# Weights' factor inside the split, four small operations off VectorE, wide filler products

## The chip, the cores and the metric

The kernel runs on one core of a Trainium2 chip. Its engines each work through a queue of their own, in order: TensorE (PE; its weight loads are listed as PEld), VectorE (DVE), ScalarE (ACT), GpSimd (POOL), and SyncE (SP), which only issues transfers here. The metric is the device time of one launch in microseconds (us); lower is better.

## What is computed

Three stages follow each other. The first is attention over chunks of 32 queries (4 batches, 8 heads, 768 positions, 64 columns a head), each chunk seeing 8 memory keys and 56 neighbours. Its result, 3072 tokens of 512 columns, goes through a layer with SoLU (h times softmax of h), a layer norm with a factor `g_ln` for each of 1024 inner columns, and then through a second layer with 2048 inner columns.

```python
a = np.exp(scores - np.max(scores, axis=-1, keepdims=True))
a = a / (np.sum(a, axis=-1, keepdims=True) + 1e-09)
...
h = x @ w_in
e = np.exp(h - h_max)
solu = h * (e / (np.sum(e, axis=-1, keepdims=True) + 1e-09))
ln = (solu - mu) / np.sqrt(var + 1e-06) * g_ln
x = ln @ w_out
...
h = x @ w2_in
out = (h * np.clip(h + 3.0, 0.0, 6.0) / 6.0) @ w2_out
```

The weights arrive as 64-bit numbers; the kernel makes 32-bit ones of them with bit operations.

## The kernel before

The tokens are cut into 24 tiles of 128. Each big product is made of three fp32r products: an operand is split into a high part (`hi`, the value rounded to fp32r) and a low part (`lo`, the rest), and hi times hi, hi times lo and lo times hi are summed.

The work of the first stages is written out by hand as lists of steps. `FIRST` holds everything up to the point where the pipeline is full (tiles 0 to 6 through SoLU, up to tile 8 through attention, and the conversion of the first layer's weights, `w1_*`, and of the SoLU layer's second weights, `wo_*`). `BODY` is one period of the loop over tiles 7 to 23, `LAST` and `CHANGE` lead into the last layer. An entry `name:args` calls a function that issues instructions; every engine takes its instructions in the order of the list, so an instruction waits for all those that stand ahead of it on its engine.

The steps that matter here, for a tile i:

- `k_p:i,half` transposes the keys of a tile on TensorE, two pairs of heads in a call; each pair takes a transpose of 128 rows (`kn`) and one of 24 rows (`km`). `k_e` (mostly ScalarE) copies the result to `kT`, a single buffer until tile 9, so it waits for the scores of the tile before. `q_p`, `q_e` do the same for the queries (`qb`).
- `s_p` makes the scores (PSUM tile `sc`), `s_max`, `s_sub`, `s_exp`, `s_sum` the softmax up to 1/(sum + 1e-9), `s_norm` multiplies by it (`pn`), `p_p` transposes that, `p_e` copies it to `pb`, `v_p` multiplies by the values, `x_h` and `x_l` split the result, `m1` makes h.
- `ln_max`, `ln_exp`, `ln_den`, `ln_solu`, `ln_mean`, `ln_sq`, `ln_var`, `ln_pow`, `ln_norm` are SoLU and the layer norm; `ln_p` transposes, `ln_h` and `ln_l` split, `m2` multiplies by the second weights.
- `wo_abs`, `wo_hold`, `wo_bits` convert a block of the second weights, `wo_g` multiplies it by `g_ln`, `wo_hi` and `wo_lo` split it.
- `warm:n` puts n products on TensorE whose result nobody reads; they fill waits.

Transposes and their evictions share three PSUM buffers (`tp`), the scores have one (`sc`).

Of the kernel before, what the change touches and what calls it, by code (L numbers as in the profile page):

```python
# [8 lines left out]
F32 = mybir.dt.float32  # L9
F32R = mybir.dt.float32r  # L10
# [25 lines left out]
    s_norm:1,P spread_mem_v:0,0,A q_p:3 load_q:4 k_e:3,1,A warm:2 v_p:0 w1_lo:7,D k_e:3,0,A q_e:3,1,A s_max:2 k_p:4,1
    q_e:3,0,D w1_bits:5,2 w1_hi:6,A w1_lo:6,P w1_hi:5,A w1_lo:5,P s_sub:2 x_h:0,0 x_l:0,0 load_w1:3 s_exp:2 p_p:1
    p_e:1,0,A w1_abs:1,A p_e:1,1,A s_p:3 k_p:4,0 k_e:4,0,A k_e:4,1,A m1:0,1,0 s_sum:2 s_norm:2,D q_p:4 p_p:2 load_v:1
    w1_hold:1,P load_w1:2 s_max:3 s_sub:3 q_e:4,1,A m1:0,1,1 w1_bits:1,0 w1_abs:3,D w1_bits:1,1 w1_bits:1,2 w1_hi:1,D
    load_k:5 w1_lo:1,D q_e:4,0,A spread_mem_v:1,0,A s_p:4 spread_mem_v:1,64,A v_p:1 x_h:1,0 load_q:5 w1_hold:3,P  # L40
    w1_bits:3,0 p_e:2,0,A w1_bits:3,1 consts w1_abs:2,A x_l:1,0 w1_bits:3,2 w1_hold:2,D load_v:2 load_wo:7 p_e:2,1,A
    m1:0,0,0 w1_bits:2,0 w1_bits:2,1 early_open m1:1,0,0 w1_bits:2,2 w1_hi:3,A w1_hi:2,A w1_lo:2,P load_k:6 s_exp:3
    w1_lo:3,D k_p:5,1 k_e:5,1,D q_p:5 q_e:5,0,A k_p:5,0 k_e:5,0,A q_e:5,1,A s_max:4 load_g s_sum:3 s_norm:3,D m1:1,1,0
    s_sub:4 s_exp:4 m1:0,0,1 load_wo:4 ln_max:0 ln_exp:0 s_sum:4 ln_den:0 ln_solu:0 v_p:2 s_p:5 wo_abs:7,A s_edge:5
    wo_abs:4,A wo_hold:7,D x_h:2,0 k_p:6,1 m1:1,0,1 x_l:2,0 k_e:6,1,D load_q:6 load_wo:5 wo_hold:4,D ln_mean:0 p_p:3
# [1334 lines left out]
```

## Time and profile before

| | |
|---|---|
| median of 3 runs | 867.32 us (866.62 to 868.14) |
| the profiled execution, its own time | 867.68 us |
| its span, first to last instruction | 865.9 us |
| TensorE busy | 858.0 us (99%) |
| VectorE busy | 747.1 us (86%) |
| ScalarE busy | 469.7 us (54%) |
| GpSimd busy | 259.3 us (30%) |
| mean granted TensorE clock | 0.996 of 2.4 GHz |

The busy time of TensorE is made of modelled ends of pipelined matmuls, so that 99% says only that it has hardly a gap; how fast it goes through its work is read from the distance of the starts. Times in the timeline are counted from the first instruction.

### The profile page before, as it was taken

The page shows a single profiled execution, that of the slowest core. Times are in us where ns is not written, and L with a number is a line of the kernel's source. Part 1 is how long each engine was busy: PE and PEld are TensorE (multiplying, and loading weights), DVE is VectorE, ACT ScalarE, POOL GpSimd, SP SyncE. Part 2 cuts the span into 40 slices and gives each one's busy share as a digit, 9 for nine tenths or more (in the row PEclk, how much of TensorE's full clock was granted, in tenths as well). Part 3 has the DMA queues.
Part 4 walks back from the last instruction along what each step waited for, and adds up shares of the span by engine and source line. Part 5 has one row for each costly group of instructions (what it writes and reads, how often), then busy time and mean ns, then how long its engine had stood idle before and what let it go on. Part 6 is the DMA issues. An engine that isn't in the chain of part 4 may idle for free.

```text
span 865.9 us, 20130 instructions
## 1 busy us (share of the span) xinstructions
PE 858.0 (99%) x7513; PEld 811.9 (94%) x7513; DVE 747.1 (86%) x1599; ACT 469.7 (54%) x865; POOL 259.3 (30%) x228
## 2 busy tenths in 40 slices
...
GB/s 239 188 219 160 72 144 225 236 230 302 240 275 224 268 274 231 145 163 228 251 191 148 225 136 207 178 173 226 240 262 255 166 135 142 158 141 135 140 141 62
DMA packets 184014, 168.27 MB, mean 194 GB/s; under 512 B 107116, under 2 KB 154220, under 8 KB 183916
## 3 DMA queue, kind: packets, MB, share of 16 engines
...
q10 hardware_dynamic: 288, 0.26, 0.1%
...
## 4 chain that ended last, share of the span: by engine, by line
PE 88%; DVE 6%; ACT 2%; DMA 2%; issue 1%; SPq 0%; DVEq 0%; ACTq 0%
PE acc L903 25%; PE acc L990 24%; PE m L694 15%; PE h L609 12%; PE tp L666 3%; PE sc L522 3%; PE tp L578 2%; PE tp L560 1%; PE tp L509 1%; PE tp L494 1%; DMA w1raw<-in_moe_w_in_dram 1%; DMA b_ll<-b_d 1%; PE tp L480 1%; DMA f_z<-g 1%; ACT e L644 0%
## 5 line engine op out<-in xcount | busy, mean ns | idle before, releaser
L694 PE MATMUL m<-lnh,wo 128*128 128x384 f32 x512 | 138.5, 344 | 0.0
L938 ACT ACTIVATE f_s<-f_e,constants 128x512 f32<-128x512 f32 x96 | 68.0, 720 | 74.2 <-DVE f_e L931 60.4
L609 PE MATMUL h<-w,xh 128*128 128x512 f32 x336 | 106.4, 398 | 0.0
L694 PEld LDWEIGHTS m<-lnh,wo 128*128 128x128 f32 x512 | 91.7, 188 | 0.2
L694 PE MATMUL m<-lnl,wo 128*128 128x384 f32 x256 | 88.0, 344 | 0.0
L311 POOL TENSOR_SCALAR w2t<-w2t 128x512 f32<-128x512 f32 x30 | 58.8, 1961 | 53.6 <-ACT w2t L304 53.6
L609 PEld LDWEIGHTS h<-w,xh 128*128 128x128 f32 x336 | 60.9, 188 | 11.6 <-ACT lnh L337 0.3
L941 DVE SCALAR_TENSOR_TENSOR f_s<-f_s,f_e 128x512 f32<-128x512 f32 x96 | 68.5, 722 | 0.9 <-ACT f_s L938 0.9
L609 PE MATMUL h<-w,xl 128*128 128x512 f32 x168 | 65.7, 391 | 0.0
L298 ACT ACTIVATE kT<-tp 128x448 f32<-128x448 f32 (+3 forms) x59 | 23.6, 455 | 60.3 <-PE tp L494 52.3
L694 PEld LDWEIGHTS m<-lnl,wo 128*128 128x128 f32 x256 | 48.2, 189 | 0.1
L793 ACT ACTIVATE b_qb<-f_kn 128x384 fp32r<-128x384 f32 (+1 forms) x48 | 27.6, 576 | 28.2 <-DVE f_kn L969 14.5
L609 PEld LDWEIGHTS h<-w,xl 128*128 128x128 f32 x168 | 31.5, 188 | 6.9
L341 DVE TENSOR_TENSOR lnl<-tp,lnh 128x512 fp32r<-128x512 f32 x41 | 26.7, 685 | 10.6 <-ACT lnh L337 10.6
L298 ACT ACTIVATE qb<-tp 64x512 f32<-64x512 f32 x46 | 27.3, 593 | 14.9 <-PE tp L509 14.3
L935 DVE TENSOR_TENSOR f_e<-acc,f_e 128x512 f32<-128x512 f32 x48 | 32.9, 686 | 2.2 <-PE acc L903 0.4
L927 DVE TENSOR_TENSOR f_e<-acc,f_e 128x512 f32<-128x512 f32 x48 | 32.9, 685 | 1.2 <-PE acc L903 0.3
L552 POOL TENSOR_TENSOR pn<-pe,ast 128x512 f32<-128x512 f32 x19 | 20.0, 1053 | 45.8 <-DVE ast L548 31.1
L624 ACT ACTIVATE e<-h,lst 128x1024 f32<-128x1024 f32 x24 | 26.4, 1100 | 12.1 <-DVE lst L618 11.9
L618 DVE TENSOR_REDUCE lst<-h 128x1 f32<-128x1024 f32 x24 | 29.2, 1217 | 3.5 <-PE h L609 3.4
L644 ACT ACTIVATE e<-so,lst 128x1024 f32<-128x1024 f32 x24 | 27.4, 1143 | 8.1 <-DVE lst L640 8.1
L635 DVE SCALAR_TENSOR_TENSOR so<-h,lst,e 128x1024 f32<-128x1024 f32 x24 | 30.7, 1278 | 0.7 <-PE tp L666 0.5
...
## 6 DMA issues: line engine op xcount, KB each, us to landing
...
```

What stands on the lines that cost most here:

```text
L298: ACT.activation(out=out, in_=in_, func=AF.Copy)
L311: ENG[eng].tensor_scalar(out=tf, in0=tf, scalar1=U_LO, scalar2=U_HI, op0=ALU.max, op1=ALU.min)
L609: PE.matmul(h[:, f], a[:, kt], w[kt][:, f * 512:(f + 1) * 512], start=n == 0, stop=n == 3 * NKT - 1)
L618: DVE.tensor_reduce(st_t[i][:, 2:3], h_t[i].rearrange("p a b -> p (a b)"), axis=AX.X, op=ALU.max, negate=True)
L635: DVE.scalar_tensor_tensor(out=so_t[i], in0=h_t.pop(i).rearrange("p a b -> p (a b)"), scalar=st[:, 5:6], in1=e_t[i], op0=ALU.mult, op1=ALU ...
L694: PE.matmul(acc, w[fc // 2][:, fc % 2, dc * P:(dc + 1) * P], a[:, fc], start=n == 0, stop=n == len(todo) - 1)
L903: PE.matmul(o, w[wl][:, c * P:(c + 1) * P], x[xl][:, c], start=m == 0 and half == 0, stop=m == 5, skip_group_check=True)
L927: DVE.tensor_tensor(c_of(n)[1], bank(n % 2, 2), wide(c_of(n)[0][:, 1]), ALU.add)
L935: DVE.tensor_tensor(c, bank(n % 2, 3), c, ALU.add)
L938: ACT.activation(out=g_of(n)[k], in_=c_of(n)[k], func=AF.Relu, bias=three, scale=1.0)
L941: DVE.scalar_tensor_tensor(out=g_of(n)[k], in0=g_of(n)[k], scalar=6.0, in1=c_of(n)[k], op0=ALU.min, op1=ALU.mult)
L990: PE.matmul(bank(t % 2, k)[:, half], g[al][:, G_BLOCK[p]], b_op[j, p][bl], start=j == 0 and m == 0 and half == 0, stop=j == NU - 1 and m = ...
```

## The change

Four things change. (1) The factor `g_ln` is no operation of its own any more: `wo_hi` is a ScalarE copy with the factor as its scale, and `wo_lo` a VectorE operation that multiplies by the factor and subtracts the high part; all `wo_hi` are on ScalarE now and all `wo_lo` on VectorE (three of eight were on GpSimd). (2) Four small operations of every tile leave VectorE: the 1e-9 of the attention's sum goes to GpSimd (`s_sum`), and its reciprocal becomes a step of its own, `s_rec`, right ahead of `s_norm`; the 1e-9 of SoLU's sum goes to ScalarE, behind the exponential (`ln_exp`); the mean goes to ScalarE (`ln_mean`), the variance to GpSimd (`ln_var`). (3) `k_p` issues its two transposes of 128 rows first and then the two of 24 rows. (4) `warm` issues fp32r products 512 columns wide instead of fp32 transposes of 128 columns, of a copy of the identity that ScalarE makes at the start; there are 37 of them instead of 61, and seven calls of `warm:1` stand between the transposes of tiles 2 to 4, where `FIRST` had a single `warm:2`.

```diff
-    s_max:0 s_sub:0 s_exp:0 s_sum:0 load_w1:5 load_q:1 warm:16 q_p:1 q_e:1,1,A s_norm:0,D w1_hi:0,P k_p:1,0 warm:13
+    s_max:0 s_sub:0 s_exp:0 s_sum:0 load_w1:5 load_q:1 warm:8 q_p:1 q_e:1,1,A s_rec:0 s_norm:0,D w1_hi:0,P k_p:1,0
...
-    def wo_g(u):
-        t, g = raw["wo", u][1].bitcast(F32), raw["wo", u][4]
-        DVE.tensor_scalar(out=t, in0=t, scalar1=g, scalar2=None, op0=ALU.mult)
-
-    def wo_hi(u, eng):
-        copy(raw["wo", u][2], raw["wo", u][1].bitcast(F32), eng)
-
-    def wo_lo(u, eng):
+    def wo_hi(u):
         d, t, hi, lo, g = raw["wo", u]
-        ENG[eng].tensor_tensor(lo, t.bitcast(F32), hi.bitcast(F32), ALU.subtract)
+        ACT.activation(out=hi, in_=t.bitcast(F32), func=AF.Copy, scale=g)
+
+    def wo_lo(u):
+        d, t, hi, lo, g = raw["wo", u]
+        DVE.scalar_tensor_tensor(out=lo, in0=t.bitcast(F32), scalar=g, in1=hi.bitcast(F32),
+                                 op0=ALU.mult, op1=ALU.subtract)
...
-        for j in range(2):
-            h = 4 * half + 2 * j
+        heads = [4 * half + 2 * j for j in range(2)]
+        for j, h in enumerate(heads):
             PE.transpose(pt[:, j, 0:P], kn[i % 2][:, h:h + 2].rearrange("t h d -> t (h d)"), ident)
+        for j, h in enumerate(heads):
             PE.transpose(pt[:, j, P:P + KR], km[i % 2][0:KR, h:h + 2].rearrange("t h d -> t (h d)"),
                          ident[0:KR, 0:KR])
...
         DVE.tensor_reduce(st[:, 1], p_t[i], axis=AX.X, op=ALU.add)
-        DVE.tensor_scalar(out=st[:, 2], in0=st[:, 1], scalar1=1e-9, scalar2=None, op0=ALU.add)
-        DVE.reciprocal(st[:, 1], st[:, 2])
+        POOL.tensor_scalar(out=st[:, 2], in0=st[:, 1], scalar1=1e-9, scalar2=None, op0=ALU.add)
+
+    def s_rec(i):
+        DVE.reciprocal(st_a[i][:, 1], st_a[i][:, 2])
...
+        ACT.activation(out=st[:, 4:5], in_=st[:, 3:4], func=AF.Copy, bias=1e-9)
 
     def ln_den(i):
         st = st_t[i]
-        DVE.tensor_scalar(out=st[:, 4:5], in0=st[:, 3:4], scalar1=1e-9, scalar2=None, op0=ALU.add)
         DVE.reciprocal(st[:, 5:6], st[:, 4:5])
...
-        DVE.tensor_scalar(out=st[:, 7:8], in0=st[:, 6:7], scalar1=-1.0 / FF, scalar2=None, op0=ALU.mult)
+        ACT.activation(out=st[:, 7:8], in_=st[:, 6:7], func=AF.Copy, scale=-1.0 / FF)
...
-        DVE.tensor_scalar(out=st[:, 9:10], in0=st[:, 8:9], scalar1=1.0 / FF, scalar2=1e-6,
-                          op0=ALU.mult, op1=ALU.add)
+        POOL.tensor_scalar(out=st[:, 9:10], in0=st[:, 8:9], scalar1=1.0 / FF, scalar2=1e-6,
+                           op0=ALU.mult, op1=ALU.add)
...
+        ident_r = T("s1", [P, P], F32R, "ident_r")
+        ACT.activation(out=ident_r, in_=ident, func=AF.Copy)
+
         def warm(n):
             t = idle.tile([P, 4, P], F32, tag="w", name="idle")
             for j in range(n):
-                PE.transpose(t[:, j % 4], ident, ident)
+                PE.matmul(t, ident_r, ident_r.unsqueeze(1).to_broadcast([P, 4, P]), start=True, stop=True)
...
             if ok(m + 1) and m > STEADY:
+                s_rec(m + 1)
                 s_norm(m + 1, "P")
```

What the lists make of it on the engines is shown at three places. The first is TensorE's queue in `FIRST`, from the filler behind `mem_p:2` to `mem_p:1` (`kn`, `km`: `k_p:2,0`; `q_raw`: `q_p:2`; `mk`: the memory keys). Before:

```order
L1050 MATMUL idle<-ident 128x128 x3
L480 MATMUL tp<-ident,kn_131 128x128
L481 MATMUL tp<-ident,km 128x24
L480 MATMUL tp<-ident,kn_131 128x128
L481 MATMUL tp<-ident,km 128x24
L509 MATMUL tp<-ident,q_raw 128x128 x4
L467 MATMUL tp<-ident,mk 128x8 x4
```

And of the change at the same place:

```order
L1054 MATMUL idle<-ident_r 128x512 x2
L478 MATMUL tp<-ident,kn_131 128x128 x2
L480 MATMUL tp<-ident,km 128x24 x2
L1054 MATMUL idle<-ident_r 128x512
L508 MATMUL tp<-ident,q_raw 128x128 x4
L465 MATMUL tp<-ident,mk 128x8 x4
```

The transposes of like height stand together, and a wide filler has come between `k_p` and `q_p`.

The second is VectorE's queue in `FIRST` at tile 2, from `x_l:0` to `s_max:3` (`pe` are the exponentials, `ast` the small sums). Before:

```order
L341 TENSOR_TENSOR xl<-tp,xh 128x512
L546 TENSOR_REDUCE ast<-pe 128x8
L547 TENSOR_SCALAR ast<-ast 128x8
L548 RECIPROCAL ast<-ast 128x8
L552 TENSOR_TENSOR pn<-pe,ast 128x512
L534 TENSOR_REDUCE ast<-sc 128x8
```

And of the change:

```order
L341 TENSOR_TENSOR xl<-tp,xh 128x512
L545 TENSOR_REDUCE ast<-pe 128x8
L549 RECIPROCAL ast<-ast 128x8
L553 TENSOR_TENSOR pn<-pe,ast 128x512
L533 TENSOR_REDUCE ast<-sc 128x8
```

The addition has left the queue, and the reciprocal, which needs it back from GpSimd, is the very next entry.

The third is VectorE's queue in one period of `BODY`, from `s_sum` to the entry behind `ln_max` (`w2t`: conversion of the last layer's weights). Before:

```order
L546 TENSOR_REDUCE ast<-pe 128x8
L547 TENSOR_SCALAR ast<-ast 128x8
L548 RECIPROCAL ast<-ast 128x8
L315 TENSOR_SCALAR w2t<-w2t 128x512
L618 TENSOR_REDUCE lst<-h 128x1
L318 SCALAR_TENSOR_TENSOR w2t<-w2raw,w2t 128x512
```

And of the change:

```order
L545 TENSOR_REDUCE ast<-pe 128x8
L315 TENSOR_SCALAR w2t<-w2t 128x512
L619 TENSOR_REDUCE lst<-h 128x1
L549 RECIPROCAL ast<-ast 128x8
L318 SCALAR_TENSOR_TENSOR w2t<-w2raw,w2t 128x512
```

The reciprocal has moved behind `ln_max`, since `s_rec` is issued where `s_norm` stands in the list.

## Rows read from the trace of the kernel before

**Rows 1.** Windows by stage: length, busy of each engine, PEclk, DMA share, GB/s.

```profile
20.00:33.00 13.00, 12.86 (x137) 9.70 (x136) 10.28 (x20) 10.85 (x20) 6.28 (x5) 0.74 0.81 194
33.00:73.00 40.00, 39.67 (x382) 31.28 (x381) 38.64 (x80) 30.31 (x53) 20.76 (x16) 1.00 0.86 207
...
112.00:382.00 270.00, 270.00 (x2344) 245.07 (x2343) 209.71 (x408) 147.94 (x280) 135.63 (x129) 1.00 0.78 233
```

**Rows 2.** Timeline of TensorE at 22 us: start, length, engine, line, instruction.

```profile
22.37 0.47 PE L480 MATMUL tp<-ident,kn 128*128 128x128 f32 x1
```

**Rows 3.** Timeline at 72 to 73 us, VectorE's ln_norm:1 and TensorE's queue.

```profile
71.96 0.99 DVE L659 TENSOR_SCALAR so<-so,lst 128x1024 f32<-128x1024 f32 x1
...
71.83 0.62 PE L609 MATMUL h<-w,xh 128*128 128x512 f32 x2
72.28 0.39 PE L609 MATMUL h<-w,xl 128*128 128x512 f32 x1
73.10 0.63 PE L666 MATMUL tp<-ident,so 128*128 128x128 f32 x4 [0.42 <-DVE so L659]
```

**Rows 4.** Timeline of TensorE at 42 us, transposes at the full clock.

```profile
42.25 0.33 PE L480 MATMUL tp<-ident,kn 128*128 128x128 f32 x1
42.51 0.24 PE L481 MATMUL tp<-ident,km 24*128 24x24 f32 x1
42.68 0.66 PE L509 MATMUL tp<-ident,q_raw 128*128 128x128 f32 x4
43.17 0.27 PE L480 MATMUL tp<-ident,kn 128*128 128x128 f32 x1
```

**Rows 5.** Groups by source line: ns shortest/median/longest; and three groups of small operations.

```profile
L654 POOL TENSOR_TENSOR lst<-lst,constants x24: 548/560/1063, 55.2 to 378.4; 128x1 f32<-128x1 f32 x24
...
L1039 POOL MEMSET constants<- 128x1 f32 x1 | 0.1, 93 | 0.0
L629 DVE TENSOR_SCALAR lst<-lst 128x1 f32<-128x1 f32 x24 | 3.6, 152 | 23.6 <-ACT e L624 23.6
L1029 ACT ACTIVATE constants<-ident 128x1 f32<-128x1 f32 x1 | 0.2, 203 | 0.0
```

**Rows 6.** Timeline of VectorE, attention's sums of tile 0 and of tile 2.

```profile
15.03 0.69 DVE L546 TENSOR_REDUCE ast<-pe 128x8 f32<-128x512 f32 x1 [0.70 <-ACT pe L542]
...
16.14 0.20 DVE L548 RECIPROCAL ast<-ast 128x8 f32<-128x8 f32 x1
...
31.82 0.68 DVE L546 TENSOR_REDUCE ast<-pe 128x8 f32<-128x512 f32 x1
...
32.74 0.20 DVE L548 RECIPROCAL ast<-ast 128x8 f32<-128x8 f32 x1
33.05 0.93 DVE L552 TENSOR_TENSOR pn<-pe,ast 128x512 f32<-128x512 f32 x1
```

**Rows 7.** Timeline of ScalarE from 24 to 31 us.

```profile
24.18 1.71 ACT L298 ACTIVATE v<-v 8x768 f32<-8x768 f32 x2
26.99 0.98 ACT L298 ACTIVATE kT<-tp 128x448 f32<-128x448 f32 x2 [1.11 <-PE sc L522]
...
30.59 0.60 ACT L337 ACTIVATE xh<-tp 128x512 fp32r<-128x512 f32 x1
```

**Rows 8.** Timeline at 92 us, ScalarE's second p_e:6 and TensorE's v_p:6.

```profile
91.76 0.59 ACT L298 ACTIVATE pb<-tp 64x512 f32<-64x512 f32 x1
...
92.41 1.15 PE L578 MATMUL tp<-pb,v 128*64 128x64 f32 x32
```

**Rows 9.** Timeline of one period of the loop: reciprocal, entry behind ln_max, s_norm, load for p_p.

```profile
220.06 0.20 DVE L548 RECIPROCAL ast<-ast 128x8 f32<-128x8 f32 x1
...
221.62 0.68 DVE L318 SCALAR_TENSOR_TENSOR w2t<-w2raw,w2t 128x512 uint32<-128x512 uint32 x1
...
220.44 1.04 POOL L552 TENSOR_TENSOR pn<-pe,ast 128x512 f32<-128x512 f32 x1 [2.20 <-DVE ast L548]
...
223.50 0.53 PEld L560 LDWEIGHTS tp<-ident,pn 128*128 128x128 f32 x4
```

More of the change, by code (lines that the diff above doesn't have):

```diff
@@ L36 @@
[L36 to L45, printed above, removed]
@@ L56 @@
-    ln_l:1,1,1 wo_bits:0,1 q_e:7,1,A wo_bits:0,2 ln_norm:2 ln_p:2,0 wo_g:0 ln_max:4 wo_hi:7,A wo_hi:0,A m1:3,0,1
-    q_e:7,0,D s_sum:6 v_p:5 wo_bits:2,0 s_norm:6,D ln_exp:4 ln_den:4 s_p:7 ln_l:1,0,1 ln_h:2,0,1 ln_l:2,0,1 x_h:5,1
-    x_l:5,1 ln_max:3 wo_bits:2,1 ln_p:2,1 ln_solu:4 k_p:8,0 k_p:8,1 ln_exp:3 ln_den:3 k_e:8,1,A wo_bits:2,2
-    wo_hold:3,D wo_g:5 ln_mean:4 ln_h:2,1,1 load_wo:6 wo_lo:0,D ln_solu:3 early_close ln_sq:4 ln_mean:3 wo_hi:1,A
-    m1:5,0 k_e:8,0,A wo_g:2 ln_sq:3 wo_hi:2,A p_p:6 m1:5,1 wo_bits:3,0 load_q:8 wo_g:4 wo_bits:3,1 wo_lo:1,D ln_var:3
@@ new lines @@
+    m1:1,0,1 x_l:2,0 k_e:6,1,D load_q:6 load_wo:5 wo_hold:4,D ln_mean:0 p_p:3 s_rec:4 s_norm:4,P p_e:3,0,A m1:1,1,1
+    ln_max:1 q_p:6 ln_sq:0 wo_bits:7,0 ln_var:0 ln_pow:0 q_e:6,0,A wo_abs:5,D k_mem:6,D m1:2,0,0 q_e:6,1,A wo_hold:5,P
+    k_p:6,0 load_wo:0 wo_bits:4,0 s_max:5 m1:2,1,0 ln_exp:1 wo_abs:0,D k_e:6,0,A m1:2,1,1 p_e:3,1,A wo_bits:4,1
+    wo_hold:0,P load_v:3 v_p:3 x_h:3,1 ln_den:1 x_l:3,1 p_p:4 load_wo:1 ln_norm:0 ln_p:0,0 m1:2,0,1 wo_bits:4,2
+    p_e:4,0,A p_e:4,1,A wo_bits:5,0 load_v:4 wo_abs:1,A s_sub:5 s_p:6 s_exp:5 wo_bits:7,1 wo_bits:7,2 ln_h:0,0,1
@@ new lines @@
+    ln_solu:1 v_p:4 x_h:4,1 ln_mean:1 wo_hold:1,D ln_p:0,1 wo_bits:5,1 ln_l:0,0,1 s_edge:6 ln_max:2 s_sum:5 x_l:4,1
+    s_rec:5 s_norm:5,P load_k:7 k_p:7,0 ln_exp:2 m1:3,1,0 k_e:7,0,D ln_den:2 ln_h:0,1,1 ln_l:0,1,1 ln_sq:1 s_max:6
+    ln_solu:2 load_k:8 k_p:7,1 ln_var:1 ln_pow:1 load_wo:2 wo_abs:2,A wo_bits:1,0 m1:3,0,0 wo_bits:1,1 wo_bits:0,0
+    p_p:5 load_q:7 p_e:5,1,A m1:4,1,0 ln_mean:2 wo_bits:1,2 load_wo:3 ln_sq:2 ln_norm:1 load_v:5 m1:4,0,0 s_sub:6
+    ln_p:1,0 k_e:7,1,A q_p:7 wo_abs:3,A wo_hold:2,P ln_var:2 m1:4,0,1 p_e:5,0,A ln_pow:2 wo_bits:5,2 s_exp:6
```

61 lines of the change are left out of this document (33 added, 28 removed).

## The prediction

> **What bounds the kernel now.** I read the busy times by stage first. From 112 to 382 us TensorE is busy for 270.00 of 270 us, and between 33 and 73 us it lacks a third of a microsecond in 40 [rows 1]. So from about 30 us on the time is TensorE's own work, and a change can only (a) make that work shorter, (b) let TensorE come earlier to that point, or (c) make it wait. The one place there where it waits for long is 73.10 us: `ln_p:1,0` needs `ln_norm:1`, which VectorE began at 71.96 [rows 3]. VectorE is busy for 38.64 of the 40 us before that [rows 1]: there two engines run neck and neck, and VectorE is the one that arrives last. What TensorE gains ahead of 73 us is therefore kept only as far as VectorE comes earlier too; what it gains behind 73 us is kept whole. The third view is the early stretch: from 20 to 33 us the mean granted clock is 0.74 [rows 1], and the timeline shows it fall at 22.37 us: a transpose of 128 rows that takes 0.33 us at 42 us takes 0.47 [rows 2, 4]. That is the 1.2 GHz level in place of 2.4; ahead of the fall TensorE had run transposes, with only one set of score products among them.
>
> **The change, part by part.** The sum is made against the profiled execution (867.68 us), and 0.36 us are taken off at the end for the median of 867.32. The unknown in most terms is a, the length of a 128x8 or 128x1 addition on GpSimd. The trace has none. The nearest rows are a fill of 128x1 at 93 ns and a power of 128x1 at 548 to 1063 ns, median 560 [rows 5]; a power is more work than an addition, a fill is less (it reads nothing), so I take a = 0.3 us, between 0.1 and 0.56. The round trip VectorE, GpSimd, VectorE adds two crossings; from the reciprocal's end at 220.26 to `s_norm` on GpSimd at 220.44 one is 0.18 us [rows 9], so a round trip is 0.18 + 0.3 + 0.15 = 0.63 us. Before, the reciprocal began 0.24 us behind the reduction's end (31.82 + 0.68 to 32.74), at tile 0 0.42 us (15.72 to 16.14) [rows 6].
>
> On this rests the one rule of the Trainium skill that I weigh. The rows show 560 ns for one column of a power on GpSimd against 152 ns for one column of an addition on VectorE [rows 5]. The GPSIMD Engine Reference, section 3.1, names two software dispatch hops for every GpSimd instruction where VectorE has one, so by it small operations are the wrong ones to move there. With a at 0.56 the sum below would end at about 867.3 instead of 866.5.
>
> *Up to 33 us: -0.5.* At tile 0 the round trip delays `s_norm:0`, `p_p:0` and with them ScalarE by 0.63 - 0.42 = 0.2. ScalarE is then without a gap until 25.89, where it waits 1.11 us: `k_e:3,1` may overwrite `kT` only when the scores of tile 2, at half clock, are done (26.99) [rows 7]. A filler should cost what a fp32r product of 512 columns costs, 0.23 us (two take 0.62 us, one 0.39 [rows 3]). If the fillers hold the clock, the two `k_p:3`, each with its filler, take 0.9 us apiece from 22.6, the scores about half of the time they take at the lower clock, 1.1 us, and are done at 25.5, while ScalarE is free at 25.89 + 0.2 = 26.1. So `k_e:3,1` starts 0.9 us earlier, and ScalarE's and VectorE's work up to `x_h:0` (30.59) with it; TensorE's `v_p:0` needs the buffer that this `k_e` frees and is done by 28, well ahead of the new `x_h:0` at 29.7. Then `s_sum:2` has no cover for its round trip: +0.39. That leaves -0.5 for the `s_norm` at 33.05 [rows 6]. With a from 0.1 to 0.56 it is -0.9 to 0. The later start of the fillers at the top (they need ScalarE's copy, about a microsecond later than now) lies ahead of a wait of VectorE for the first weights and costs nothing; without that cover it would be that microsecond.
>
> *33 to 73 us, VectorE: -0.2.* Eight small operations (1e-9 of tiles 0 to 2, mean of 0 to 2, variance of 0 and 1) leave; each lasts 0.15 us [rows 5], but overlaps the next one, so I count 0.1: -0.8. The 1e-9 of tile 4 gains nothing, as VectorE waits there for the exponential anyway. Against it stand the round trips of tile 3 (+0.39) and tile 5 (+0.2; its reduction waits longer now, as tile 0's did). Tile 4's `s_rec` has two long operations as its cover. Bounds by a: -0.6 to +0.3. In the same stretch TensorE gets 1.6 us from eight `k_p` (next paragraph), which only makes its wait at 73 us longer.
>
> *`k_p`: -0.8 kept.* At the full clock a pair goes from its 128-row start to its 24-row start in 0.26 us and on to the next 128-row start in 0.17 [rows 4]; four transposes of 128 rows in a run take 0.49, so 0.12 each. Two pairs cost 0.86 now; grouped, 0.12 + 0.26 + 0.12 + 0.17 at most, 0.2 less a call. Twenty calls would be 4 us; only the four behind 73 us (tiles 8 and 9) are kept: -0.8 us. Whether a 24-row transpose behind another is as short as that no row shows; if the switch back costs twice, half is left.
>
> *ScalarE at 85 to 92 us: +0.3.* Between the transposes of tile 8 and `v_p:6` ScalarE is without a gap, and `v_p:6` starts 0.06 us behind its `p_e:6` [rows 8]. Two means now lie in that run; the nearest row, a 128x1 copy, lasts 203 ns [rows 5], the next instruction starting a little before its end: 2 x 0.15. Behind 73 us VectorE loses the eight factor multiplications and gets three more `wo_lo`; this is relief without a price, for TensorE does not wait for it there.
>
> *The loop: +0.4.* In each period `s_rec` now follows `ln_max`. The entry behind `ln_max` began at 221.62; without the addition and the old reciprocal that is 221.29, plus 0.2 for the mean that ScalarE runs ahead of its square, whose result opens VectorE's run. So the reciprocal goes from 220.06 to about 221.5, `s_norm` from 220.44 to 221.9, its end to 222.9; TensorE's load for `p_p` stands at 223.50 [rows 9]. About 0.4 us is left of 2.0. The order hides the move in the usual period, but one period of those shown by the trace has 1 us less room and the last one 0.6 less: I allow 0.4 us for them. From 382 us on nothing is changed.
>
> Sum: -0.5 - 0.2 - 0.8 + 0.3 + 0.4 = -0.8: 866.9 us for the profiled execution, **866.5 us** for the median.
>
> **Rivals.** (B) *VectorE does not hold TensorE back at 73 us.* All that TensorE gains would count: 3.0 us in the cold stretch net of the new fillers, 1.4 for the eight `k_p` with one filler, and the 0.58 of lateness at 73.10. Then the time is 867.3 - 5 - 0.1 = 862.2; if VectorE follows half way, 864.6. For it: its list gets shorter with every tile. Against it: 38.64 of 40 us busy, and two uncovered round trips.
> (C) *The clock falls all the same.* Then each filler costs 0.46 us, more than the grouping saves; `v_p:0` comes 0.7 later instead of earlier, and the sum up to 33 us is +1.1 instead of -0.5: 868.1. For it: the sets of real products at that place are as sparse as before. Against it: 18 of the 37 fillers stand between the scores of tile 0 and `k_p:3`, the ten microseconds ahead of the fall, and each streams 512 columns.
> (D) *`p_p` waits in every period of the loop*, the rival on the other side. The margin is 0.4 us and shrinks with the variance's length on GpSimd, which stands between `w2_hold` and the power there, ahead of `ln_norm`. It decides at a small operation of some 0.7 us in each place: the power's longest row is 1.06. At 0.25 us a period for 13 periods, and the round trips dearer by as much: 867.3 + 3.2 - 0.2 = 870.3.
>
> **How the numbers follow.** Forecast 0.43, B 0.22, C 0.19, D 0.16. The forecast's own range is 865.3 to 867.5. The range reaches from half of B to D: 863.9 to 870.0. A measurement of this kernel tells 0.2% (1.7 us) from no change, so faster means under 865.6 and slower over 869.05: faster is B and the forecast's lower end, 0.31; slower is most of D and the upper end of C, 0.20; the same, 0.49.
>
> **What would show it.** A granted clock of 1.00 from 20 to 33 us, and `k_e:3,1` at about 26.1 instead of 26.99 (C if not). A longer wait of TensorE for `ln_norm:1` than 0.42 us, at about 72.3 (B if it is gone). GpSimd's additions between 0.1 and 0.56 us. In the loop `s_norm` 1.4 us later and no wait at `p_p` (D if there is one). I am wrong if VectorE's 40 us behave otherwise than by its list, or if a small GpSimd operation is far outside its two rows.

## The result, and the profile after

The changed kernel takes 872.36 us (median of 4 runs, 871.43 to 872.95) against 867.01 us of the kernel before, measured beside it: 1.0059 of its time, with a 95% interval of 1.0041 to 1.0076. That is slower by 0.6%, where 866.5 us and no change were forecast, and it lies above the range (863.9 to 870.0) and above every rival (D: 870.3). The profiled execution takes 871.43 us, 3.8 us more than the one of before.

The windows by stage of the changed kernel, columns as in [rows 1]:

```profile
20.00:33.00 13.00, 11.15 (x142) 8.06 (x140) 11.27 (x21) 10.18 (x20) 6.71 (x5) 1.00 0.72 176
33.00:73.00 40.00, 38.51 (x381) 30.19 (x380) 37.37 (x69) 31.22 (x58) 21.10 (x22) 1.00 0.86 211
73.00:112.00 39.00, 36.18 (x268) 30.71 (x268) 33.90 (x53) 31.03 (x59) 18.95 (x20) 0.96 0.33 82
```

And the one window of the kernel before that [rows 1] leaves out:

```profile
73.00:112.00 39.00, 38.82 (x342) 33.38 (x343) 37.71 (x75) 29.64 (x53) 18.23 (x15) 1.00 0.39 99
```

From 20 to 33 us the clock is now held (1.00 instead of 0.74). But TensorE lacks 1.5 us in the 40 up to 73 us and 2.8 in the 39 behind it, where it lacked 0.3 and 0.2. VectorE's busy time goes down (37.37 for 38.64, 33.90 for 37.71), and TensorE waits more for it. Where that comes from shows in two timelines. First the rows of the kernel before at three places that the prediction did not look at: GpSimd's splits of the first layer's weights and VectorE's next two conversions at 17 us, GpSimd's two splits `ln_l` at 77 us, and VectorE's `ln_solu:4` (with the read of its accumulator) ahead of TensorE's `m1:5`. The last two rows are the transposes on both sides of tile 9's `k_p`:

```profile
12.86 0.61 POOL L300 CAST w<-w1raw 128x512 fp32r<-128x512 f32 x1 [8.42 <-DVE w1raw L321]
13.56 2.51 POOL L384 TENSOR_TENSOR w<-w1raw,w 128x512 fp32r<-128x512 f32 x2
...
16.98 0.42 DVE L306 TENSOR_SCALAR w1raw<-w1raw 128x512 uint32<-128x512 uint32 x1
17.44 0.43 DVE L311 TENSOR_SCALAR w1raw<-w1raw 128x512 f32<-128x512 f32 x1
...
77.43 2.54 POOL L341 TENSOR_TENSOR lnl<-far,lnh 128x512 fp32r<-128x512 f32 x2 [2.62 <-ACT lnh L337]
...
83.35 1.27 DVE L635 SCALAR_TENSOR_TENSOR so<-h,lst,e 128x1024 f32<-128x1024 f32 x1
84.55 0.08 DVE L635 DVE_READ_ACCUMULATOR so<-h,lst,e 128x1 f32 x1
...
84.78 2.99 PE L609 MATMUL h<-w,xx 128*128 128x512 f32 x12
...
118.03 0.60 PE L666 MATMUL tp<-ident,so 128*128 128x128 f32 x4
...
129.01 0.60 PE L509 MATMUL tp<-ident,q_raw 128*128 128x128 f32 x4
```

And the timeline of the changed kernel, by place: tile 0 and the same splits and conversions, `k_e:3,1`, tiles 5 and 1 up to 75 us, the addition of tile 6 with what stands behind it, `s_norm:6` and `ln_solu:4` ahead of `m1:5`, the transposes on both sides of tile 9's `k_p`, and one period of the loop:

```profile
15.79 0.25 POOL L546 TENSOR_SCALAR ast<-ast 128x8 f32<-128x8 f32 x1 [11.35 <-DVE ast L545]
16.10 0.61 POOL L300 CAST w<-w1raw 128x512 fp32r<-128x512 f32 x1
16.80 3.02 POOL L384 TENSOR_TENSOR w<-w1raw,w 128x512 fp32r<-128x512 f32 x2
...
17.18 1.49 DVE L306 TENSOR_SCALAR w1raw<-w1raw 128x512 uint32<-128x512 uint32 x1
18.71 1.39 DVE L311 TENSOR_SCALAR w1raw<-w1raw 128x512 f32<-128x512 f32 x1
...
27.80 0.94 ACT L298 ACTIVATE kT<-tp 128x448 f32<-128x448 f32 x2
...
33.94 0.90 DVE L553 TENSOR_TENSOR pn<-pe,ast 128x512 f32<-128x512 f32 x1
...
67.78 0.25 POOL L546 TENSOR_SCALAR ast<-ast 128x8 f32<-128x8 f32 x1 [0.68 <-DVE ast L545]
68.11 1.31 POOL L341 TENSOR_TENSOR xl<-far,xh 128x512 fp32r<-128x512 f32 x1
69.37 1.05 POOL L553 TENSOR_TENSOR pn<-pe,ast 128x512 f32<-128x512 f32 x1
...
70.48 0.66 PE L561 MATMUL tp<-ident,pn 128*128 128x128 f32 x4 [1.06 <-POOL pn L553]
74.78 0.63 PE L667 MATMUL tp<-ident,so 128*128 128x128 f32 x4 [0.89 <-DVE so L660]
...
81.61 0.36 POOL L546 TENSOR_SCALAR ast<-ast 128x8 f32<-128x8 f32 x1 [1.20 <-DVE ast L545]
82.04 1.27 POOL L341 TENSOR_TENSOR lnl<-far,lnh 128x512 fp32r<-128x512 f32 x1
...
82.24 1.63 DVE L553 TENSOR_TENSOR pn<-pe,ast 128x512 f32<-128x512 f32 x1
...
83.35 0.60 ACT L335 ACTIVATE far<-tp 128x512 f32<-128x512 f32 x1 [0.86 <-POOL lnl L341]
...
86.43 1.27 DVE L636 SCALAR_TENSOR_TENSOR so<-h,lst,e 128x1024 f32<-128x1024 f32 x1
...
87.86 4.58 PE L610 MATMUL h<-w,xx 128*128 128x512 f32 x12 [1.93 <-DVE lst L631]
...
122.34 0.60 PE L667 MATMUL tp<-ident,so 128*128 128x128 f32 x4
...
132.80 0.60 PE L508 MATMUL tp<-ident,q_raw 128*128 128x128 f32 x4
...
225.55 0.19 DVE L549 RECIPROCAL ast<-ast 128x8 f32<-128x8 f32 x1
...
225.92 1.29 POOL L553 TENSOR_TENSOR pn<-pe,ast 128x512 f32<-128x512 f32 x1 [1.30 <-DVE ast L549]
...
227.61 0.53 PEld L561 LDWEIGHTS tp<-ident,pn 128*128 128x128 f32 x4
```

Read it from the top. The addition of 1e-9 (15.79) is the first thing in GpSimd's queue after its fills, and GpSimd sits in front of it for 11.35 us until VectorE's reduction ends. Behind it in the same queue stand the high part `w1_hi:0` and the low parts `w1_lo:0` and `w1_lo:4`, which ran from 12.86 to 16.07 before, in an empty stretch. Now they run from 16.10 to 19.82, beside VectorE's conversions of the next block, which take 1.49 and 1.39 us instead of 0.42 and 0.43: 2.0 us of VectorE are gone at once. That is why `k_e:3,1` starts at 27.80 and not at 26.1, though the clock is held, and why the `s_norm:2` that stood at 33.05 [rows 6] is at 33.94.

At tile 5 the same happens again: the addition waits for the reduction, `x_l:4` behind it starts at 68.11 (before: 66.06), `s_norm:5` at 69.37, and `p_p:5` waits 1.06 us. `ln_p:1,0`, at 73.10 in [rows 3], is at 74.78 after a wait of 0.89. At tile 6 it happens a third time: the addition (81.61) now parts the splits `ln_l:1,1,1` and `ln_l:1,0,1`, which ran back to back from 77.43 before. The second of them starts at 82.04, lies beside `s_norm:6`, which takes 1.63 us (0.68 before), and ScalarE waits 0.86 us for it (83.35). And `m1:5` waits 1.93 us; the profile names a reciprocal that ends at the same time, what it needs is the buffer that `ln_solu:4` reads (86.43): in all 18 traces `m1:5` begins 0.15 us behind the read of that operation's accumulator. In the kernel before `ln_solu:4` was done at 84.63 and `m1:5` began at 84.78, so there was no reserve at all. After that wait TensorE's granted clock is below 1.00 (window 73 to 112: 0.96), and the twelve products of `m1:5` take 4.58 us instead of 2.99.

By its starts, against those of the kernel before, TensorE is 0.50 us late at 63 us, 1.68 at `ln_p:1,0`, 1.70 at the transposes ahead of `m1:5` (82.53 before, 84.23 now), 4.68 at `p_p:6` behind it (87.60 before, 92.28 now) and 3.79 behind tile 9's `k_p` (129.01 and 132.80).

### The profile page after: what moved, and what is told of

Read it like the earlier page. It is cut to its first block, busy times and chain, and to the rows that moved or that the text cites. A ratio compares the mean times of both kernels' runs of the same rounds, so it can differ in the third digit from the quotient of the medians.

```text
span 869.7 us, 20021 instructions
## 1 busy us (share of the span) xinstructions
PE 855.2 (98%) x7489; PEld 807.6 (93%) x7489; DVE 743.6 (86%) x1497; ACT 481.0 (55%) x915; POOL 274.2 (32%) x273
## 4 chain that ended last, share of the span: by engine, by line
PE 86%; DVE 8%; DMA 2%; ACT 1%; issue 1%; POOL 1%; SPq 0%; DVEq 0%; ACTq 0%; POOLq 0%
PE acc L904 25%; PE acc L991 24%; PE m L695 15%; PE h L610 13%; PE tp L667 3%; PE sc L521 2%; PE tp L579 2%; PE tp L561 1%; PE tp L508 1%; PE tp L493 1%; DMA w1raw<-in_moe_w_in_dram 1%; DMA b_ll<-b_d 1%; DVE w1raw L321 1%; DMA f_z<-g 1%; DVE pn L553 0%
## 5 line engine op out<-in xcount | busy, mean ns | idle before, releaser
L610 PEld LDWEIGHTS h<-w,xh 128*128 128x128 f32 x336 | 61.0, 188 | 12.1 <-POOL w L384 0.7
L794 ACT ACTIVATE b_qb<-f_kn 128x384 fp32r<-128x384 f32 (+1 forms) x48 | 27.7, 576 | 28.8 <-DVE f_kn L970 13.5
L321 DVE SCALAR_TENSOR_TENSOR w2t<-w2raw,w2t 128x512 uint32<-128x512 uint32 x32 | 32.3, 1009 | 1.1
L553 POOL TENSOR_TENSOR pn<-pe,ast 128x512 f32<-128x512 f32 x19 | 23.4, 1232 | 26.2 <-DVE ast L549 24.5
```

What stands on the lines that cost most here:

```text
L321: DVE.scalar_tensor_tensor(out=t, in0=words(raw64)[1], scalar=29, in1=t, op0=ALU.logical_shift_right, op1=ALU.bitwise_or)
L610: PE.matmul(h[:, f], a[:, kt], w[kt][:, f * 512:(f + 1) * 512], start=n == 0, stop=n == 3 * NKT - 1)
```

## The experiments

All times are compared with runs of the kernel before that were made in the same batch. The ratio of the times and its 95% interval are the measurement's own; 0.1% is 0.87 us. e1 to e5 are the changed kernel with one thing undone, b1 to b9 the kernel before with one part of the change, c1 to c3 look for a faster one.

The last column is worked out from each trace: for every line and shape of VectorE its shortest row is taken, and what all its rows up to 112 us last beyond that is summed up. I call it the stretch of VectorE. The kernel before has 7.0 us of it.

| run | what it is | ratio | interval | stretch, us |
|---|---|---|---|---|
| the change | | 1.0059 | 1.0041 to 1.0076 | 12.2 |
| e1 | change, attention's addition back on VectorE | 1.0032 | 1.0020 to 1.0044 | 9.4 |
| e2 | change, GpSimd's splits ahead of the addition | 1.0036 | 1.0020 to 1.0052 | 10.4 |
| e3 | change, SoLU's three operations back | 1.0061 | 1.0047 to 1.0076 | 12.5 |
| e4 | change, factor an operation of its own again | 1.0051 | 1.0038 to 1.0065 | 13.2 |
| e5 | change, attention's addition and reciprocal back | 1.0012 | 0.9998 to 1.0026 | 9.3 |
| b1 | before, order of `k_p` | 1.0000 | 0.9986 to 1.0014 | 9.4 |
| b2 | before, wide fillers | 1.0017 | 1.0003 to 1.0030 | 7.0 |
| b3 | before, order of `k_p` and wide fillers | 1.0015 | 1.0004 to 1.0025 | 9.1 |
| b4 | before, factor inside the splits | 1.0007 | 0.9995 to 1.0019 | 7.0 |
| b5 | before, attention's part | 1.0068 | 1.0049 to 1.0086 | 13.5 |
| b7 | before, attention's addition on GpSimd alone | 1.0034 | 1.0021 to 1.0046 | 12.1 |
| b8 | before, late reciprocal alone | 1.0020 | 1.0005 to 1.0034 | 9.0 |
| b9 | before, SoLU's three operations moved | 1.0018 | 1.0004 to 1.0032 | 8.3 |
| c1 | before, without the two additions of 1e-9 | 0.9981 | 0.9971 to 0.9991 | 7.5 |
| c2 | c1 with the order of `k_p` | 0.9973 | 0.9963 to 0.9984 | 8.3 |
| c3 | c2 with the factor inside the splits | 0.9984 | 0.9974 to 0.9993 | 5.3 |

**e1: the addition back on VectorE.**

```diff
-        POOL.tensor_scalar(out=st[:, 2], in0=st[:, 1], scalar1=1e-9, scalar2=None, op0=ALU.add)
+        DVE.tensor_scalar(out=st[:, 2], in0=st[:, 1], scalar1=1e-9, scalar2=None, op0=ALU.add)
```

> The changed kernel with one thing undone: the 1e-9 of the attention's sum is added on VectorE again, right behind the reduction; the reciprocal stays where the change puts it. Theory Q (GpSimd's queue): the addition stands in GpSimd's queue ahead of three splits of the first layer's weights and of the split of tile 4, waits there for VectorE's reduction and holds them back (the first runs from 16.10 instead of 12.86), and they then lie beside VectorE's conversions and stretch them (1.49 and 1.39 us instead of 0.43). Q expects the splits at 12.9 us again, the conversion at 17 us 0.4 to 0.5 us long, the start of ln_norm:1 before 72.5 us, and 867 to 869.5 us. Theory S (ScalarE): the loss comes from ScalarE, which has got the means, the additions of SoLU and three more high parts; S expects a gain of at most 0.7 us, 871.5 to 872.5 us.

Measured: 1.0032. From 1.0059, that is 0.27% or 2.3 us gained, more than theory S allows and less than Q said. The two intervals just touch (1.0044 and 1.0041); e3, made in the same batch with the addition on GpSimd, is clear of e1 (1.0047 to 1.0076). In the trace (its execution is 1.7 us above e1's median) the conversion at 16.85 us lasts 0.42 us, as Q expected; but `ln_norm:1`, which Q wanted before 72.5, starts at 75.54. What was gained up to 30 us went again by 65 us: TensorE, now early, waits for transfers (0.9 us for `v`, 0.4 for `q_raw`, 0.3 for `kn`), and VectorE waits 1.1 us for a block of the second weights and has two conversions of 1.75 and 1.76 us beside GpSimd.

**e2: the same operations, another order in GpSimd's queue.**

```diff
-    s_max:0 s_sub:0 s_exp:0 s_sum:0 load_w1:5
+    s_max:0 s_sub:0 s_exp:0 w1_hi:0,P w1_lo:0,P w1_lo:4,P s_sum:0 load_w1:5
...
-    s_edge:6 ln_max:2 s_sum:5 x_l:4,1
+    s_edge:6 ln_max:2 x_l:4,1 s_sum:5
```

> The changed kernel with the same instructions on the same engines; only in the list the three splits on GpSimd (w1_hi:0, w1_lo:0, w1_lo:4) are issued ahead of s_sum:0, and x_l:4 ahead of s_sum:5, so that the additions no longer stand ahead of them. Q expects most of what e1 gains: 868 to 870 us (the addition of tile 0 itself has to wait some 0.4 us for the third split), conversions at 17 us short again. S expects no change, 871.5 to 872.9 us. If the addition costs by its round trip alone and not by what it holds back, there is no gain either.

Measured: 1.0036. Nothing is taken away, only the queue differs, and about as much comes back as in e1; but e2's interval overlaps the change's (1.0041 to 1.0076), so the times alone do not settle it. In e2's timeline GpSimd's splits, VectorE's two conversions and `k_e:3,1` stand so:

```profile
12.45 0.61 POOL L300 CAST w<-w1raw 128x512 fp32r<-128x512 f32 x1 [8.01 <-DVE w1raw L321]
13.15 2.53 POOL L384 TENSOR_TENSOR w<-w1raw,w 128x512 fp32r<-128x512 f32 x2
15.76 0.25 POOL L546 TENSOR_SCALAR ast<-ast 128x8 f32<-128x8 f32 x1
...
16.89 0.42 DVE L306 TENSOR_SCALAR w1raw<-w1raw 128x512 uint32<-128x512 uint32 x1
17.34 0.43 DVE L311 TENSOR_SCALAR w1raw<-w1raw 128x512 f32<-128x512 f32 x1
...
25.70 0.94 ACT L298 ACTIVATE kT<-tp 128x448 f32<-128x448 f32 x2
```

So what the addition costs at tile 0 is what it holds back, and that these splits then run beside VectorE's conversions, not its own 0.25 us: with the round trip still there, `k_e:3,1` comes at 25.70, near the 26.1 of the prediction, instead of 27.80. The waits of TensorE from 30 to 112 us show where e2 is stopped instead (waiting engine, tile, line, what ended it: us, times, longest; e2's profiled execution is 4.9 us above its median, so it shows the places and not the sum):

```profile
PE h L610 <- DVE lst L631: 1.9, 1, 1.9
PE tp L579 <- DMA v<-in_v_dram: 1.7, 2, 0.9
```

Keys and queries (`kn`, `q_raw`) take 0.7 us more each. The first row is `m1:5`: e2 reorders the queue at tiles 0 and 5 only, and at tile 6 the addition still stands ahead of `ln_l:1,0,1`.

**e3 and e4: the other two parts undone.**

```diff
-        ACT.activation(out=st[:, 7:8], in_=st[:, 6:7], func=AF.Copy, scale=-1.0 / FF)
+        DVE.tensor_scalar(out=st[:, 7:8], in0=st[:, 6:7], scalar1=-1.0 / FF, scalar2=None, op0=ALU.mult)
```

(e3; the 1e-9 and the variance likewise. e4 has `wo_g`, `wo_hi` and `wo_lo` and their places as before.)

> The changed kernel with the three small operations of SoLU and layer norm (the 1e-9, the mean, the variance) back on VectorE. S expects 869 to 870.5 us: ScalarE's chain ahead of m1:5 is shorter by four small operations of 0.1 to 0.2 us, and the wait of m1:5 (1.93 us) shrinks by at least 0.8. Q expects 871.5 to 873.5 us: VectorE gets 0.3 us a tile back, which it is short of.

> The changed kernel with the factor of the second weights as an operation of its own again, its splits on the engines of before. The trace after shows VectorE wait 3.2 us for high parts of ScalarE, the longer of the two 2.4 us at about 105 us. S expects 869 to 871 us, as that wait and the three high parts leave. Q expects no change within 0.7 us, 871.6 to 873 us, since the loss stands at 88 us already and TensorE does not wait between 93 and 208 us.

Measured: 1.0061 and 1.0051, both within the interval of the change's own 1.0059. S falls: neither relief for ScalarE brings anything that can be told from nothing, and `m1:5` waits 1.92 and 1.93 us in them, where S expected at least 0.8 less in e3. (ScalarE has one high part more in the change and not three: seven of the eight were there before.)

**e5 and b5: the attention's part undone, and alone.**

```diff
     def s_rec(i):
-        DVE.reciprocal(st_a[i][:, 1], st_a[i][:, 2])
+        pass
```

(e5, together with e1's line and the reciprocal behind it in `s_sum`; b5 is the reverse on the kernel before.)

> The changed kernel with the attention's part undone: 1e-9 and reciprocal on VectorE right behind the reduction, as before; all other parts of the change stay. Theory Q+L: the addition on GpSimd costs about 2.5 us by what it holds back (e1 and e2 gain about that), and the late reciprocal (behind ln_max) another 1 to 2 us by waits at p_p in the loop (e1 shows 0.64 us at 213.6 and 0.37 at 306.4, e2 0.65, 1.10 and 0.50); it expects no wait at p_p in the loop and a ratio of 1.000 to 1.002 to before. Theory W (the filler and the order of k_p bring TensorE early and the loss is theirs): no change against e1, a ratio of 1.003.

> The kernel before with the attention's part of the change alone: 1e-9 on GpSimd, the reciprocal as a step of its own ahead of s_norm. Q+L: slower by 3 to 5 us (ratio 1.0035 to 1.006), with the splits on GpSimd at 16.1 us and the conversions at 17 us near 1.4 us long. W: within 1 us of before (0.999 to 1.001).

Measured: 1.0012 for e5, 1.0068 for b5. Without this part the change can hardly be told from the kernel before; this part alone is as slow as the whole change. In b5 TensorE waits for GpSimd's `s_norm` in the loop, and it does in no period of before. The waits of TensorE from 112 to 382 us, of b5 and of b8 (the next but one):

```profile
PE tp L562 <- POOL pn L554: 2.1, 2, 1.9
```

```profile
PE tp L562 <- POOL pn L554: 1.0, 2, 0.6
```

**b1 and b3: the order of `k_p`, without and with the fillers.**

```diff
+        heads = [4 * half + 2 * j for j in range(2)]
+        for j, h in enumerate(heads):
             PE.transpose(pt[:, j, 0:P], kn[i % 2][:, h:h + 2].rearrange("t h d -> t (h d)"), ident)
+        for j, h in enumerate(heads):
             PE.transpose(pt[:, j, P:P + KR], km[i % 2][0:KR, h:h + 2].rearrange("t h d -> t (h d)"),
```

> The kernel before with the two transposes of 128 rows issued first in k_p, alone. My prediction's term: two calls behind 73 us count with 0.2 us each for tiles 8 and 9, so 0.8 us faster, 0.9990 to 0.9998. If the gain of the early calls is kept as well, as VectorE does not hold TensorE back: 2 to 4 us faster, 0.995 to 0.998. W expects no gain, 1.000.

> The kernel before with the order of k_p and the wide fillers (their counts and places as in the change), no small operation moved and the weights' factor as before. My prediction's terms: clock held at 22 to 29 us, which VectorE gives back at 73 us: 0.997 to 1.000. Q+L: the same, about 0.998, since neither of the two costs anything. W: slower, 1.002 to 1.004, as TensorE then meets transfers that have not landed at 42 to 65 us (e1: 0.9 us for v, 0.4 for q_raw, 0.3 for kn).

Measured: 1.0000 and 1.0015. b1 can be told neither from W's 1.000 nor from the prediction's 0.9990 to 0.9998; b3 (1.0004 to 1.0025) lies above what the prediction's terms and Q+L said and reaches only the lower end of what W said. In b1's trace TensorE is early by 3.1 us at `p_p:1` and late by 0.7 at `ln_p:1,0`: the whole gain of the cold stretch goes before 73 us, as the prediction's reason has it, and a little more. b1 is at 1.00 in the window from 20 to 33 us with the old fillers, so the clock did not fall there in that execution, though nothing but the order of the transposes had changed.

**b7 and b8: the attention's part taken apart.**

```diff
-        DVE.tensor_scalar(out=st[:, 2], in0=st[:, 1], scalar1=1e-9, scalar2=None, op0=ALU.add)
+        POOL.tensor_scalar(out=st[:, 2], in0=st[:, 1], scalar1=1e-9, scalar2=None, op0=ALU.add)
         DVE.reciprocal(st[:, 1], st[:, 2])
```

(b7. b8 leaves the addition on VectorE and moves only the reciprocal, as the change does.)

> The kernel before with the 1e-9 of the attention's sum added on GpSimd, and the reciprocal on VectorE right behind it, where it was. Against b5 (ratio 1.0068) it leaves out the late reciprocal. Q+L: the held-back splits and their collisions with VectorE remain, and the round trip now stands bare on VectorE in every tile; in FIRST as slow as b5 (conversions at 17 us near 1.4 us long, VectorE's excess over the shortest rows some 12 us up to 112 us instead of 7), no wait at p_p in the loop: 1.003 to 1.006. If the late reciprocal is the main cost: 1.000 to 1.002.

> The kernel before with the reciprocal as a step of its own right ahead of s_norm (in the loop behind ln_max), the addition left on VectorE. Q+L: waits at p_p in the loop as in e1 (0.6 and 0.4 us) and 1 to 2 us in all, ratio 1.001 to 1.003, and up to 112 us the same as before. If the late reciprocal costs only together with GpSimd's addition: 1.000.

Measured: 1.0034 and 1.0020; together they make 0.54% of b5's 0.68%. b7 has the stretch of VectorE (12.1 us) and no wait at `p_p` in the loop, b8 has the waits (1.0 us by the profile's count, 1.6 by the distances of TensorE's starts) and only a part of the stretch (9.0). In b8's trace (1.6 us above its median) TensorE is 2.0 us late at 73 us already, where no difference had been expected, so about half of its loss is not the loop's.

b7 has nearly all of its loss at `m1:5`: TensorE is 0.3 us late ahead of it and 3.2 behind it, and the rows are those of the change at tile 6:

```profile
80.23 0.25 POOL L547 TENSOR_SCALAR ast<-ast 128x8 f32<-128x8 f32 x1 [1.18 <-DVE ast L546]
80.56 1.28 POOL L341 TENSOR_TENSOR lnl<-far,lnh 128x512 fp32r<-128x512 f32 x1
...
86.38 4.57 PE L609 MATMUL h<-w,xx 128*128 128x512 f32 x12 [1.31 <-DVE lst L629]
```

In the six traces with the attention's addition on GpSimd (the change, e2, e3, e4, b5, b7) `m1:5` waits 1.31 to 1.94 us, in the other twelve 0.03 to 0.96.

**b2, b4 and b9: the other three parts one by one.**

```diff
-                PE.transpose(t[:, j % 4], ident, ident)
+                PE.matmul(t, ident_r, ident_r.unsqueeze(1).to_broadcast([P, 4, P]), start=True, stop=True)
```

(b2, with the change's counts and places of `warm`; b4 is the change's `wo_hi` and `wo_lo`, b9 the lines of e3 the other way round.)

> The kernel before with the wide fillers alone (their counts and places as in the change). The clock is expected at 1.00 from 20 to 33 us. If what TensorE gains there is given back by 73 us and each filler adds 0.23 us: 0.999 to 1.001. If the fillers are what made b3 slower than b1 (1.0015 against 1.0000): 1.001 to 1.003.

> The kernel before with the weights' factor inside the splits alone (all high parts on ScalarE, all low parts on VectorE). My prediction gave this no price: 0.999 to 1.001. The trace after shows VectorE wait 2.4 us at 105 us for a high part; if TensorE needs what stands behind it, 1.001 to 1.003.

> The kernel before with the three small operations of SoLU and layer norm moved alone (1e-9 and mean to ScalarE, variance to GpSimd). My prediction: VectorE gains 0.1 us for each up to 73 us, ScalarE costs 0.3 at 85 to 92 us, so 0.9990 to 1.0005. If these moves, too, cost by waits of VectorE for ScalarE and GpSimd: 1.001 to 1.003.

Measured: 1.0017, 1.0007 and 1.0018. In b2's trace the fillers lose at their start: they wait for ScalarE's copy of the identity (2.47 us for 1.35 before), take 0.43 us apiece (ten in 4.63 us) where the prediction took 0.23, though the granted clock from 2.4 to 7 us is 1.00 in the profile, and VectorE then waits 2.28 us for tile 0's transposes:

```profile
2.47 4.63 PE L1053 MATMUL idle<-ident_r 128*128 128x512 f32 x10 [2.47 <-ACT ident_r L1048]
...
10.96 0.19 DVE L300 COPY kmT<-tp 128x32 f32<-128x32 f32 x1 [2.28 <-PE tp L467]
```

Its reduction `s_max:0` is at 13.99 there and at 12.92 before. In the change's own trace it is at 12.90, so this loss of b2 is not one that the change pays there. In b9 the place is `ln_norm:3` (its profiled execution is 1.6 us below its median and shows the place, not the sum; TensorE is 1.1 us early ahead of it and 0.7 late at 103 us). The variance on GpSimd sits in its queue for 5.68 us until ScalarE's square is done, and the split behind it, which was done at 88.04 before, starts only at 90.08; the powers come to 91.98 (90.80 before), and `ln_norm:3` to 92.57 (91.85 before). It is the queue again, with another operation in front:

```profile
89.41 0.58 POOL L649 TENSOR_SCALAR lst<-lst 128x1 f32<-128x1 f32 x1 [5.68 <-ACT e L644]
90.08 1.55 POOL L341 TENSOR_TENSOR lnl<-far,lnh 128x512 fp32r<-128x512 f32 x1
...
92.57 0.81 DVE L659 TENSOR_SCALAR so<-so,lst 128x1024 f32<-128x1024 f32 x1 [2.10 <-POOL lst L654]
```

**c1, c2 and c3: a faster version.** The additions of 1e-9 are left out, which changes nothing in 32-bit numbers: each sum holds exp(0) = 1.

```diff
-        DVE.tensor_scalar(out=st[:, 2], in0=st[:, 1], scalar1=1e-9, scalar2=None, op0=ALU.add)
-        DVE.reciprocal(st[:, 1], st[:, 2])
+        DVE.reciprocal(st[:, 1], st[:, 1])
...
-        DVE.tensor_scalar(out=st[:, 4:5], in0=st[:, 3:4], scalar1=1e-9, scalar2=None, op0=ALU.add)
-        DVE.reciprocal(st[:, 5:6], st[:, 4:5])
+        DVE.reciprocal(st[:, 5:6], st[:, 3:4])
```

> The kernel before without the two additions of 1e-9: each sum holds exp(0) = 1, so in 32-bit numbers the addition changes nothing; VectorE gets rid of two small operations per tile, and nothing is added anywhere. If VectorE's list is what counts: 16 additions of 0.1 to 0.2 us up to 92 us, of which the wait at 73 us (0.58 us) and that at 84.8 keep a part, 0.9980 to 0.9995. If what counts is which of VectorE's operations fall beside GpSimd's (collisions), a shift of a few tenths can go either way: 0.999 to 1.003 with the excess above 7 us.

> c1 with the two transposes of 128 rows issued first in k_p. The calls of tiles 8 and 9 should keep 0.2 to 0.25 us each, as in b1, where tile 9 kept 0.51: 0.997 to 0.9995 by VectorE's list; 0.999 to 1.003 if collisions decide.

> c2 (no additions of 1e-9, which change nothing in 32-bit numbers; the order of k_p) with the weights' factor inside the splits as well. If the fold is free relief for VectorE: 0.9960 to 0.9975, below c2 (0.9973). If it costs by waits for ScalarE: 0.998 to 1.000.

Measured: 0.9981, 0.9973 and 0.9984. All three are faster than the kernel before; c2 has the lowest median, 865.53 us, but the three intervals overlap. A window and the waits of TensorE of c2:

```profile
20.00:33.00 13.00, 10.50 (x142) 7.82 (x141) 11.20 (x19) 11.44 (x22) 7.88 (x5) 1.00 0.72 181
```

```profile
PE tp L665 <- DVE so L658: 1.0, 1, 1.0
PE h L609 <- DVE lst L629: 0.5, 1, 0.5
```

The same two places, `ln_norm:1` and `ln_solu:4`, still end TensorE's stretches. c3, with the factor inside the splits, has the least stretch of all (5.3 us) and is not faster; VectorE waits 1.7 us there for ScalarE's high parts.

## Why the prediction was wrong, point by point

**What bounds the kernel.** That VectorE arrives last at 73 us and that gains ahead of it don't count was right (b1: 3.1 us early at `p_p:1`, 0.7 late at `ln_p:1,0`), and rival B is dead. That 73.10 us was the one such place was wrong: `m1:5` at 84.78 stood 0.15 us behind `ln_solu:4`. The step that behind 73 us VectorE's relief is "without a price, for TensorE does not wait for it there" hung on that, and it failed: the wait at `m1:5` (1.93 us, and the lower clock after it) is the largest single piece of the loss, 2.98 us of TensorE's time (1.70 late ahead of it, 4.68 behind). What makes it long is the addition at tile 6, as b7 and the six traces show.

By the sum: VectorE's arrival at 73 us was to be 0.7 us earlier (-0.5 and -0.2), and TensorE is 1.68 late there; from there to 130 us -0.8 and +0.3 were forecast, and it loses 2.11 more; the loop's +0.4 came out at 0.3. So about half of the miss lies ahead of 73 us, where the next step failed, and half behind it.

**Up to 33 us: -0.5 forecast, +0.9 measured** (`s_norm:2` at 33.94). This is the other step that failed. The clock was held, so rival C is out, and the price of the addition was right: 233 to 363 ns for 128x8 and 192 to 401 for 128x1, where 0.3 was taken; the round trip was even shorter than the 0.63 us that I gave it (the reduction of tile 0 ends at 15.02 + 0.69 and the reciprocal begins at 16.07, 0.36 us later, for 0.42 before). What I left out is what stands behind the addition in GpSimd's queue, and so priced at nothing. I took only VectorE's side of the round trip and did not read GpSimd's list at that place, where three splits follow. e2's rows show the cause with nothing but the order changed. (With a at 0.56 the prediction's own bounds add up to 867.5 and not to 867.3; that plays no part in this.)

The rows also say how the two engines disturb each other: VectorE's conversion from 17.18 ends at 18.67 and needs 0.42 of its own, as if it had started at 18.25, about when the first of GpSimd's two low parts (3.02 us for both, from 16.80) is done; the next one ends at 20.10, 0.28 behind the second's end at 19.82. The Trainium skill, in SBUF — State Buffer, section "SBUF: two separate sides", says that GpSimd and some of VectorE's operations (those in a 2-port mode, and those with two SBUF inputs against a GpSimd operation that reads SBUF) share a pair of ports as an exclusive lock: whichever starts first holds it for its whole instruction while the other fully blocks. These rows agree with that better than with a slowdown in proportion, but only roughly: 0.28 us is less than the conversion's own 0.43, and no run here tests the lock by itself.

**33 to 73 us: -0.2 forecast, +0.7 measured** (`ln_norm:1` 1.58 us later, of which 0.9 was there at 33 us). The eight small operations did leave VectorE. Against them stand the held-back `x_l:4` at tile 5 and conversions that now fall beside GpSimd. The stretch of VectorE up to 112 us grows by 5.2 us, from 7.0 to 12.2, where the moved operations save 0.8 by the prediction's own count. Over the 17 kernels of the table with a trace of their own (the change included), each one above 10 us of stretch is at 1.0034 or more, and each at 9.3 or less is at 1.0020 or less. That is a relation and no proof: the two at 9.4 lie far apart (e1 at 1.0032, b1 at 1.0000), and c3 has the least of it and is not the fastest.

**`k_p`: -0.8 forecast.** The size was right: from the transposes of `ln_p` at 118.03 to those of `q_p` at 129.01 it was 10.98 us, and it is 10.46 now (122.34 to 132.80), so tile 9's two calls keep 0.52, or 0.26 a call where 0.2 was taken. Tile 8's calls lie ahead of `m1:5` and only lengthen its wait, so about 0.5 is kept and not 0.8.

**ScalarE at 85 to 92 us: +0.3.** It can't be seen behind the 2.98 us that TensorE has lost at `m1:5`. Undoing it (e3) brought nothing.

**The loop: +0.4.** The margin of about 0.4 us is there: `s_norm` at 225.92 ends at 227.21 and the load for `p_p` begins at 227.61, so 0.40 us are left. In part that is luck: by the prediction's own times (222.9 and 223.50) it is nearer 0.6, and `s_norm` takes 1.29 us here where 1.04 was taken. In three of the fifteen periods nothing was left (the load begins 0.05 us behind the end of `s_norm`), and the profiled execution pays 0.3 us for that, all of it at 212 us. But other kernels with the late reciprocal pay 1.0 us (e1), 2.2 (e2), 1.6 (b8) and 2.4 (b5) by the distances of TensorE's starts. So the mechanism of rival D was there, in single periods and not in all; b8 as a whole is at 0.20% or 1.7 us, and about half of that lies ahead of the loop in its trace.

**The costs given as nothing.** The fillers' later start was priced at nothing, as it lies ahead of VectorE's wait for the first weights. b2 shows that this cover is about 1 us and does not always hold; in the change's own trace it held. Alone the parts cost 0.68, 0.18, 0.17, 0.07 and 0.00%, together 1.10, and the whole change costs 0.59: losses ahead of the same waits can share them, which is argued and not shown.

**What stays open.** The profiled execution of the change is the fastest of its four; what the others lose beyond it (0.4 to 1.5 us) has no trace. The two slowest (872.88 and 872.95) have a mean granted clock of 1.000 and the profiled one 0.998, so the change is as slow without the lower clock behind `m1:5`; e2 and e4 wait as long there, and their clock stays at 1.00 from 73 to 112 us. How much the waits for transfers between 40 and 65 us make, and so why e1 and e2 gain less than Q expected, is not settled either, though e2's addition at tile 6 is a part of it: the transfers differ between executions by more than the waits (the load of keys at 14.9 us takes SyncE 2.12 us before, 1.22 after, 2.99 in e1), and no run here takes them out.
